# An attention and gated-product kernel: an early key tile, sums moved between engines, one reader per PSUM bank, and a verdict computed in steps

## The chip, the cores and the metric

The kernel runs on one core of one Trainium2 chip. Its time is the device time of one execution, in microseconds (us). The kernel before was timed three times: 763.4 us in the median, 762.13 at least and 764.25 at most.

## The reference

There are 4 batches, 8 heads, 768 positions and 64 elements a head; 4 positions are sinks and the window is 128. Scores are masked to the sinks and the window, the softmax and the weighted values follow, and the result, as 3072 rows of 512, goes through three weight matrices.

```python
scores = scale * np.matmul(q, k.transpose(0, 1, 3, 2))
keep = is_sink | in_window
scores = np.where(keep, scores, -1000000000.0)
a = np.exp(scores - np.max(scores, axis=-1, keepdims=True))
a = a / (np.sum(a, axis=-1, keepdims=True) + 1e-09)
x = np.matmul(a, v)                # 3072 x 512 after a transpose
out = (x @ w_a) * (x @ w_b) @ w_out    # 512x1536, 512x1536, 1536x512
```

All inputs are float32. The number of sinks and the window come as data; the kernel is written for up to 4 sinks and a window up to 128.

## The kernel before

**Split values.** Most matmuls take operands in a rounded form (`fp32r`). A value is kept as a high half and a low half, and a product takes three matmuls: high by high, high by low, low by high. ScalarE mostly makes the high half (a cast), VectorE or GpSimd the low half (value minus high half).

**Chunks.** The products run in seven chunks, c = 0 to 6. Chunk 0 takes the first block of 128 rows of every batch, whose attention `first_tiles` does with an order written out by hand (`FIRST_ORDER`); chunks 1 and 2 take two tiles of 128 rows each, chunks 3 to 6 the last four tiles of one batch each. Beside the products of a chunk runs the attention for later rows: from chunk 1 on a generator `rest()` yields small attention steps, and the products call `between()` after each group of matmuls (a slot), which takes as many steps as the table `PACE` says: chunk number, then (slots, first step, last step). So `1: (37, 0, 34)` spreads steps 0 to 34 over 37 slots. The first 20 steps of `rest()` are an exact attention for two tiles (`pipeline`, `parts_exact`); then comes `attention` for four batches with four tiles each (`parts_split`), the rows of chunks 3 to 6. Chunk 6 has no attention beside it.

**The first 40 us.** `weights`, `weight_words`, `weight_sum`, `weight_high` and `weight_low` turn each raw 64-bit weight into a float32 and then into its halves: two VectorE operations on the words, a ScalarE conversion and a sum, a ScalarE copy (high), a subtraction (low). `weight_high` (L369 to L374) also stores the float32 weight to DRAM through ScalarE's DMA queue (`send`, L1053). Instructions marked with `keep_in_program_order` stay in the order in which they are written on their engine; others, the store among them, are placed by the scheduler. From the end of chunk 0 on, `keep_order` fixes the order on TensorE, VectorE, ScalarE and GpSimd as it is written. The steps of `FIRST_ORDER` that matter here: `H0` to `H3` cast a batch's rows to `xh` (L573), `L0` to `L3` make `xl` (L577), `X` is the exponential (L530), `C` a copy (L540), `wa0`, `ra0`, `ha0`, `la0` the four stages of weight a0, and `begina`, `beginb` start the first products.

**Split attention.** A step of `attention` takes one head and one tile. `load_kq` (L424) brings a key tile for two heads and a query tile; `prep_k` and `prep_q` make their halves on GpSimd (`round` L407, `rest` L410); `scores` (L693) is two matmuls, one with `qh`, one with `ql` (L698); VectorE masks (L705, L706), ScalarE takes the exponential (L708), VectorE the sum and its reciprocal (L717, L718), ScalarE scales (L720). The key tile uses the buffer tag `pt`, which the exact attention's transposed probabilities (`ptx`) hold before. With `cold` set, the first of the four batches begins with three extra steps that load head 0, make its keys and queries, and load head 1's queries.

**Products.** Chunks 1 and 2 use `moe2`: 12 column blocks of weights a and b, then the output product (`project`, L976), whose `gh` and `gl` are made one block behind. Chunks 3 to 6 use `moe7`, a form of matrix product with seven instead of eight block products, with operands `B11`, `T1` to `T4`, `B21`, `B22` made from the chunk's rows by `make_ops` (L1113) in six stages, one stage a slot. For each pair `i` of column blocks and each kind (a, then b) there are four slots. Two PSUM banks are used: X (tag `a`) and Y (tag `b`). X is copied to SBUF by ScalarE (L1238), Y is added to it (L1242), X goes on accumulating, and then its two halves are read: its second half by VectorE into `v12` (L1248 or L1251), its first half into `first`, in kind a by ScalarE's copy (L1256), in kind b by VectorE's multiplication (L1250). The next X uses the same bank. GpSimd adds and multiplies in between (L1243, L1252, L1313) and makes `gl` (L1310); the output product is `project_piece` (L1197). The attention's scores use one PSUM bank in chunks 3 to 5 and two in chunks 1 and 2 (`roomy`).

**The verdict.** While the weights are used, `reduce_check` gathers a minimum and a sum of squares of the raw words. Near the end `verdict` (L70) compares these and the two scalars on VectorE, transposes the result with TensorE, reduces it to one flag, and `values_load` reads the flag into a register of every engine. If the flag is 0 a general path follows; here it does not run.

Of the kernel before, what the change touches and what calls it, by code (L numbers as in the profile page):

```python
# [19 lines left out]
DM, FF = 512, 1536  # L20
# [48 lines left out]

def verdict(tc, cp, ident, chk, val, gp):  # L70
# [5 lines left out]
    V.tensor_reduce(mm[:, 0:1], chk[:, :6 * NJ], axis=AX.X, op=ALU.min)  # L76
    V.tensor_reduce(mm[:, 1:2], chk[:, 6 * NJ:], axis=AX.X, op=ALU.max)
    pin(V.tensor_scalar(bad[:, 0:1], mm[:, 0:1], H_MIN, None, op0=ALU.is_ge))
    pin(V.tensor_scalar(bad[:, 1:2], mm[:, 1:2], H_SUM, None, op0=ALU.is_lt))
    pin(V.tensor_scalar(bad[:, 2:3], val[:, 0:1], 0.0, None, op0=ALU.is_ge))  # L80
    pin(V.tensor_scalar(bad[:, 3:4], val[:, 0:1], float(NS), None, op0=ALU.is_le))
    pin(V.tensor_scalar(bad[:, 4:5], val[:, 1:2], 1.0, None, op0=ALU.is_ge))
    pin(V.tensor_scalar(bad[:, 5:6], val[:, 1:2], float(P), None, op0=ALU.is_le))
    good = cp.tile([P, 2], F32, name="good")
    V.tensor_reduce(good[:, 0:1], bad[:, 0:6], axis=AX.X, op=ALU.min)
    flag = cp.tile([1, 1], I32, name="flag")
    nc.tensor.transpose(gp, good[:, 0:1], ident)
    V.tensor_reduce(flag, gp, axis=AX.X, op=ALU.min)
    return nc.values_load(flag[0:1, 0:1], min_val=0, max_val=1,
                          skip_runtime_bounds_check_because="a comparison gives 0 or 1")  # L90

# [147 lines left out]
class Fast:  # L239
# [169 lines left out]
    def rest(self, o, i, high):  # L409
        self.nc.gpsimd.tensor_tensor(o, i, high.bitcast(F32), op=ALU.subtract)  # L410

# [11 lines left out]

    def load_kq(self, places, h, tag):  # L424
        if h % 2 == 0:
            self.kr = []
            for b, t0, n, s0, nb, kw, *_ in places:
                shape, name = [P, kw], f"kr{tag}_{h}_{b}"
                kr = self.cp.tile(shape, F32, tag="pt", name=name) if kw > DM else self.io(shape, F32, name)
# [16 lines left out]
    def prep_q(self, places, h, tag, k, done):  # L446
        nq = sum(n for _, _, n, *_ in places) * P
        x = self.sp.tile([P, NT * P], F32R, tag=("qh", "ql")[k], name=f"{('qh', 'ql')[k]}{tag}_{h}")
        if k == 0:
            self.round(x[:, :nq], self.qr[:, :nq])  # L450
        else:
            self.rest(x[:, :nq], self.qr[:, :nq], done[1][:, :nq])
        return [x]
# [137 lines left out]

    def attention(self, parts, nt, new_xf, after, cold):
# [12 lines left out]
        for h in range(H + 1):  # L605
# [55 lines left out]
    def parts_split(self, segs):  # L661
# [12 lines left out]

        def load(h):
            self.load_kq(places, h, tag)

# [3 lines left out]
        def queries(h, n):  # L681
            kq[h] += self.prep_q(places, h, tag, n, kq[h])

        def values(m):
# [8 lines left out]
        def scores(h, i):  # L693
            ks, qh, ql = kq[h]
# [358 lines left out]
    def send(self, key, x, queue):  # L1053
        d = self.away[key] = self.dr.tile(list(x.shape), F32, tag="d_" + "_".join(map(str, key)),
                                          name="d_" + "_".join(map(str, key)))
        queue.dma_start(d, x)

# [59 lines left out]
    def make_ops(self, xf, tmp):  # L1117
# [15 lines left out]
        def less(o, x, y, e):  # L1133
# [75 lines left out]
    def moe7(self, c, rows, between, ahead, following, last):  # L1209
# [10 lines left out]
        for i in range(NI):  # L1220
            end = i == NI - 1
            for ki, kind in enumerate("ab"):
                if last and i == NI - 2 and ki == 0:
                    assert not self.checks and not self.unchecked
                    self.ok = self.verdict(self.ps.tile([1, P], F32, tag="s", name="gp"))
                if last and end and ki == 1:
# [6 lines left out]
                X = self.ps.tile([P, 2 * HN], F32, tag="a", name=f"X{c}_{i}{kind}")  # L1233
                lead = self.product(X[:, :HN], w("A11"), ops["B11"], True)
                self.product(X[:, HN:], w("S1"), ops["T1"], False, lead)
                if ready:
# [6 lines left out]
                self.late.append(lambda v22=v22, u2=u2, w2=w2: G.tensor_tensor(v22, u2, w2, op=ALU.add))  # L1243
                self.product(X[:, :HN], w("A12"), ops["B21"], False)
                self.product(X[:, HN:], w("S4"), ops["B22"], False)
                self.done_with(2)
                if ki == 0:
                    slot(lambda: V.tensor_tensor(v12, X[:, HN:], u2, op=ALU.add))  # L1248
                else:
                    slot(lambda: V.tensor_tensor(first, X[:, :HN], quarter(av, 0), op=ALU.mult),  # L1250
                         lambda: V.tensor_tensor(v12, X[:, HN:], u2, op=ALU.add))  # L1251
# [83 lines left out]
    def run(self, scalars, verdict):  # L1335
# [23 lines left out]
        def rest():  # L1359
            yield from self.exact_attention(chunks[1], new_xf(1), True)  # L1360
            for k, parts in enumerate(split):
                after = split[k + 1] if k + 1 < len(split) else None
                yield from self.attention(parts, NT, lambda: new_xf(k + 2), after, k == 0)

# [12 lines left out]
        self.masks(val, True)  # L1377
        self.verdict = lambda gp: verdict(val, gp)
        xs = self.new_x(B)
# [98 lines left out]
def body(tc, kT, kD, qT, vB, vS, kq0, v0, wa, wb, wo, nw, out):  # L1478
    nc = tc.nc
    with tc.tile_pool(name="const", bufs=1) as cp:  # L1480
        ident = cp.tile([P, P], F32, name="ident")
        raw = cp.tile([P, 4], I32, name="nw_raw")
        nc.scalar.dma_start(raw, nw)
        make_identity(nc, ident)
        chk = cp.tile([P, 12 * NJ], F32, name="chk")
        with ExitStack() as ctx:
            f = Fast(tc, ctx, ident, (kT, kD, qT, vB, vS, kq0, v0, wa, wb, wo), out, chk)
            val, ok = f.run(lambda: scalars_to_float(tc, cp, raw), lambda val, gp: verdict(tc, cp, ident, chk, val, gp))
        with tc.If(ok < 1, label="general"):
            general_path(tc, ident, val, kT, qT, vB, wa, wb, wo, out)  # L1490
# [62 lines left out]
```

## Time and profile before

| | us |
|---|---|
| median of three timed runs | 763.4 |
| profiled execution | 759.96 |
| its span in the trace | 758.2 |
| TensorE busy | 730.9 |
| VectorE busy | 466.6 |
| ScalarE busy | 391.6 |
| GpSimd busy | 370.5 |

The page gives each engine's busy time. TensorE's matmuls are pipelined and their ends are modelled, so a stretch without a gap can still be slower than its regular pace; for that one looks at the distance of the starts. PEld is the weight load, which runs beside the matmul. PEclk is the share of the full clock that TensorE was granted. In a wait, the name behind the arrow is what came last before the instruction could start. The products of chunk 0 run from about 28 to 150 us, chunk 1's from there to 222, chunk 2's to 297; chunks 3, 4, 5 and 6 begin near 297, 410, 528 and 646.

### The profile page before, as it was taken

To read this page: it belongs to the slowest core of one execution; us is meant where nothing else is said; L and a number is where in the kernel's file an instruction comes from. 1 tells how busy PE (TensorE), PEld (TensorE's weight loads), DVE (VectorE), ACT (ScalarE), POOL (GpSimd) and SP (SyncE) were. 2 spreads that over 40 slices of the span, in tenths; PEclk is the share of its full clock that TensorE was granted. 3 is DMA by queue.
4 is the path that set the end of the run, shared out by engine and by line. 5 is a ranking of instruction groups with operands and counts; after the bars stand their busy time and mean duration, and the time that the engine had idled before them with its cause. 6 is when DMAs were issued, how large, how long until landed. Compare 5 with 4: busy or idle time off the path is not lost.

```text
span 758.2 us, 14626 instructions
## 1 busy us (share of the span) xinstructions
PE 730.9 (96%) x4952; PEld 642.9 (85%) x4952; DVE 466.6 (62%) x1273; ACT 391.6 (52%) x1135; POOL 370.5 (49%) x390
## 2 busy tenths in 40 slices
PE   8899999999979999899999999999999999999897
PEld 6787778888869888889888888889888988889795
DVE  5799999365476758756647566646567645533222
ACT  5677776376455665555534555443465553444111
POOL 2200000035866795866735876744876633634330
PEclk9999999999999999999999999999999999999999
DMA  9989963368736587867775586876487666599551
GB/s 333 349 291 335 384 234 118 100 212 277 260 105 202 148 274 234 269 223 243 237 253 195 199 298 221 263 241 226 170 286 244 214 210 205 179 329 321 172 164 59
DMA packets 80642, 175.86 MB, mean 232 GB/s; under 512 B 8624, under 2 KB 26032, under 8 KB 80560
## 3 DMA queue, kind: packets, MB, share of 16 engines
q1 hardware_dynamic: 76960, 168.56, 66.6%
q10 hardware_dynamic: 3600, 6.30, 2.2%
q8 instruction: 41, 0.67, 0.4%
q14 instruction: 41, 0.34, 0.2%
HBM read 144.93 MB, written 29.88 MB: 231 GB/s over the span
## 4 chain that ended last, share of the span: by engine, by line
PE 78%; POOL 7%; DMA 6%; DVE 3%; ACT 3%; issue 2%; SPq 1%; ACTq 0%; POOLq 0%; DVEq 0%
PE o L1197 15%; PE b L899 7%; PE a L899 7%; PE o L926 4%; PE av L738 4%; PE s L698 4%; PE o L976 2%; PE s L807 2%; PE X_1b L1150 2%; PE X_4b L1150 2%; PE X_3b L1150 2%; PE t L726 2%; PE X_0b L1150 2%; PE X_4a L1150 2%; PE X_2a L1150 2%
## 5 line engine op out<-in xcount | busy, mean ns | idle before, releaser
L708 ACT ACTIVATE p<-p,st 128x132 f32<-128x132 f32 x128 | 51.7, 404 | 82.2 <-DVE st L706 82.0
L1197 PE MATMUL o<-r_O,gh 128*128 128x512 f32 x288 | 93.7, 406 | 0.0
L1310 POOL TENSOR_TENSOR gl<-bu,gh 128x512 fp32r<-128x512 f32 x46 | 59.3, 1290 | 52.6 <-ACT gh L1307 51.7
L720 ACT ACTIVATE p<-p,st 128x132 f32<-128x132 f32 x128 | 44.9, 398 | 39.6 <-DVE st L718 39.6
L1029 POOL TENSOR_TENSOR s_a<-s_a 128x256 f32<-128x256 f32 x4 | 2.9, 734 | 123.2 <-PE o L926 114.2
L717 DVE TENSOR_SCALAR st<-st 128x2 f32<-128x2 f32 x64 | 36.3, 567 | 42.5 <-ACT p L708 42.5
L705 DVE COPY_PREDICATED s<-own,s 128x128 f32<-128x128 uint16 x128 | 36.8, 288 | 37.9 <-PE s L698 37.7
L1197 PE MATMUL o<-r_O,gl 128*128 128x512 f32 x144 | 56.5, 392 | 0.0
L410 POOL TENSOR_TENSOR ks<-kr,ks 64x656 fp32r<-64x656 f32 x32 | 51.0, 1593 | 2.7
L1197 PEld LDWEIGHTS o<-r_O,gh 128*128 128x128 f32 x288 | 45.0, 189 | 2.6 <-issue 2.1
L1243 POOL TENSOR_TENSOR bu<-x 128x256 f32<-128x256 f32 x24 | 19.0, 792 | 55.9 <-DVE x L1242 54.2
L728 DVE TENSOR_TENSOR pt<-t,tri 128x1024 f32<-128x1024 f32 x32 | 39.1, 1221 | 5.9 <-PE t L726 5.9
L410 POOL TENSOR_TENSOR ql<-qr,qh 128x512 fp32r<-128x512 f32 x32 | 41.4, 1293 | 1.3
L899 PE MATMUL a<-x,w_a 128*128 128x256 f32 x288 | 40.1, 287 | 1.5 <-ACT x L883 1.5
L407 POOL TENSOR_SCALAR ks<-kr 64x656 fp32r<-64x656 f32 x32 | 23.6, 737 | 35.8 <-PE s L698 34.7
L706 DVE CUSTOM_DVE_ANT_0 p<-s,mg 128x132 f32<-128x132 f32 x128 | 37.8, 295 | 4.4
L698 PE MATMUL s<-ks,qh 128*128 128x260 f32 x128 | 38.2, 298 | 2.2 <-DVE st L706 2.0
L1307 ACT CAST gh<-bu 128x512 fp32r<-128x512 f32 x48 | 29.4, 613 | 19.5 <-PE o L1197 10.2
L899 PE MATMUL b<-x,w_b 128*128 128x256 f32 x288 | 39.4, 285 | 0.0
L899 PEld LDWEIGHTS a<-x,w_a 128*128 128x128 f32 x288 | 36.6, 188 | 2.7 <-ACT x L883 1.7
L698 PE MATMUL s<-ks,ql 128*128 128x260 f32 x128 | 36.4, 284 | 1.8 <-POOL ql L410 1.8
L899 PEld LDWEIGHTS b<-x,w_b 128*128 128x128 f32 x288 | 36.2, 189 | 0.4 <-issue 0.3
(480 smaller groups left out, 2258.8 us busy)
## 6 DMA issues: line engine op xcount, KB each, us to landing
r_O<-d_O SPq DMA_DIRECT2D x36, 512.0 KB, 4.2
r_H_a<-d_H_a SPq DMA_DIRECT2D x24, 512.0 KB, 5.4
r_L_a<-d_L_a SPq DMA_DIRECT2D x24, 512.0 KB, 6.1
r_H_b<-d_H_b SPq DMA_DIRECT2D x24, 512.0 KB, 5.4
r_L_b<-d_L_b SPq DMA_DIRECT2D x24, 512.0 KB, 6.0
qr<-in_qT_dram SPq DMA_DIRECT2D x32, 256.0 KB, 3.8
raw_a<-in_wa_dram SPq DMA_DIRECT2D x12, 512.0 KB, 6.8
raw_b<-in_wb_dram SPq DMA_DIRECT2D x12, 512.0 KB, 6.6
```

Source lines behind the costliest of these rows:

```text
L410: self.nc.gpsimd.tensor_tensor(o, i, high.bitcast(F32), op=ALU.subtract)
L698: nc.tensor.matmul(ps, lhsT=q[:, i * P:(i + 1) * P], rhs=ks[:, c0s[i]:c0s[i] + SW], start=n == 0, stop=n == 1)
L705: nc.vector.copy_predicated(ps[:, :P], self.own.bitcast(mybir.dt.uint16), ps[:, W:])
L706: nc.vector.tensor_tensor_reduce(out=p, in0=ps[:, :W], in1=self.mg[:, :W], scale=-0.125, scalar=BIG, op0=ALU.add, op1=ALU.min, accum_out=s ...
L708: nc.scalar.activation(p, p, AF.Exp, bias=st[:, 0:1], scale=-1.0, accum_out=st[:, 1:2])
L717: nc.vector.tensor_scalar(st[:, 2], st[:, 1], 1e-9, None, op0=ALU.add)
L720: nc.scalar.mul(p[:, k, :], p[:, k, :], st[:, 3, k:k + 1])
L728: nc.vector.tensor_tensor(self.parted(nt)[:, h % 2].rearrange("p (c m) q -> p c m q", m=2), tp.unsqueeze(2).to_broadcast(shape), self.tri. ...
L899: mm = self.nc.tensor.matmul(ps[:, cols], lhsT=w[:, ksl], rhs=x[:, kk, cols], start=start and kk == 0 and i == 0, stop=kk == NK - 1 and i ...
L1150: mm = self.nc.tensor.matmul(ps, lhsT=a[:, ksl], rhs=b[:, kk, :], start=start and kk == 0 and n == 0, stop=kk == 1 and n == 2, skip_group_ ...
L1197: self.nc.tensor.matmul(outs[t], lhsT=g[:, sl], rhs=w, start=j == 0 and n == 0, stop=j == NJ - 1 and n == 2)
L1310: (V if late else G).tensor_tensor(hl[k][1], halves[k], hl[k][0].bitcast(F32), op=ALU.subtract)
```

## The change

- The DMA that stores the first three weights (a0, b0, a1) is kept in program order on ScalarE's queue, right behind the weight's own copy.
- The first split chunk's head-0 key tile uses the buffer `xfB` instead of `pt`. Its load is issued at step 6 of `rest()`, the load of head 1's queries at step 14, the keys are made at step 17 and the queries at step 18, all beside the exact attention. The three extra steps are gone, and `PACE` is shifted by three.
- In `scores`, the first matmul of a head's first tile gets a dependence on the instruction that makes `ql`.
- In `make_ops`, one difference and two low halves (`B21`, `T4`) go from GpSimd to VectorE.
- In `moe7`, kind a's `first` is read by VectorE ahead of `v12`, in the slot after X's last products, instead of by ScalarE a product later.
- `verdict` is split into three parts: the comparisons in the slot where all stood before, the transpose and the flag two slots later, the register load at the beginning of the last pair of column blocks.

```diff
-PACE = {1: (37, 0, 34), 2: (32, 34, 64), 3: (44, 64, 105), 4: (44, 105, 146), 5: (44, 146, 187)}
+LOAD_AT = 6
+PACE = {1: (37, 0, 31), 2: (32, 31, 61), 3: (44, 61, 102), 4: (44, 102, 143), 5: (44, 143, 184)}
...
         if kind != "o":
-            self.send(("F", kind, j), self.wf[kind, j], self.nc.scalar)
+            op = self.send(("F", kind, j), self.wf[kind, j], self.nc.scalar)
+            if (kind, j) in FIRST:
+                self.tc.keep_in_program_order(op)
...
-        if cold:
-            load(0)
-            yield
-            yield
-            keys(0)
-            queries(0, 0)
-            queries(0, 1)
-            load(1)
-            yield
...
             for n, q in enumerate((qh, ql)):
-                nc.tensor.matmul(ps, lhsT=q[:, i * P:(i + 1) * P], rhs=ks[:, c0s[i]:c0s[i] + SW],
-                                 start=n == 0, stop=n == 1)
+                mm = nc.tensor.matmul(ps, lhsT=q[:, i * P:(i + 1) * P], rhs=ks[:, c0s[i]:c0s[i] + SW],
+                                      start=n == 0, stop=n == 1)
+                if i == 0 and n == 0:
+                    self.tc.add_manual_dep(mm.ins, made.ins.name, mybir.DependencyInfo(
+                        mybir.DependencyClass.Sync, mybir.DependencyReason.DATA), reason="one wait for both parts")
...
-                [low("T1", ta, V), high("T2", tb), high("T3", b12), less(b11, b21, tb, G)],
+                [low("T1", ta, V), high("T2", tb), high("T3", b12), less(b11, b21, tb, V)],
                 [low("T2", tb, V), low("T3", b12, V), high("B21", b21), high("B22", b22)],
-                [low("B22", b22, V), low("B21", b21, G), high("T4", b11)],
-                [low("T4", b11, G)]]
+                [low("B22", b22, V), low("B21", b21, V), high("T4", b11)],
+                [low("T4", b11, V)]]
...
                 if last and i == NI - 2 and ki == 0:
                     assert not self.checks and not self.unchecked
-                    self.ok = self.verdict(self.ps.tile([1, P], F32, tag="s", name="gp"))
+                    self.later(self.judge_stages())
+                if last and end and ki == 0:
+                    self.ok = self.read()
...
                 if ki == 0:
-                    slot(lambda: V.tensor_tensor(v12, X[:, HN:], u2, op=ALU.add))
+                    slot(lambda: V.tensor_copy(first, X0), lambda: V.tensor_tensor(v12, X1, u2, op=ALU.add))
...
                 self.product(Y[:, HN:], w("A22"), ops["T4"], False)
-                if ki == 0:
-                    A.copy(first, X[:, :HN])
...
+    def judge_stages(self):
+        return [[self.judge], [], [lambda: self.gather(self.ps.tile([1, P], F32, tag="s", name="gp"))]]
...
+            load, _, keys, queries = split[0][-4:]
+            begin = {LOAD_AT: lambda: load(0, "xfB"), LOAD_AT + 8: lambda: load(1), 2 * H + 1: lambda: keys(0),
+                     2 * H + 2: lambda: (queries(0, 0), queries(0, 1))}
+            for k, _ in enumerate(self.exact_attention(chunks[1], new_xf(1), True)):
+                begin.get(k, lambda: None)()
+                yield
```

## Rows read from the trace of the kernel before

**Rows 1.** The page's busy times: engine, us (share of the span), instructions.
```profile
PE 730.9 (96%) x4952; PEld 642.9 (85%) x4952; DVE 466.6 (62%) x1273; ACT 391.6 (52%) x1135; POOL 370.5 (49%) x390
```

**Rows 2.** TensorE's waits: us in total, times, the longest.
```profile
PE o L1197 <- POOL gl L1310: 4.0, 3, 1.3
PE s L698 <- DVE st L706: 2.0, 4, 1.0
PE s L698 <- POOL ql L410: 1.8, 2, 0.9
```

**Rows 3.** Timeline, 20 to 34 us: start, us, engine, line, instruction, idle before.
```profile
21.04 1.15 ACT L530 ACTIVATE p<-s,st 128x128 f32<-128x128 f32 x4 [1.98 <-DVE v L555]
...
22.71 1.49 PE L551 MATMUL av<-v,pt 128*128 128x128 f32 x11 [1.63 <-ACT pt L540]
...
31.90 0.33 ACTq L1056 DMA_DIRECT2D d_F_a<-wf_a  x1
...
32.91 0.38 PE L899 MATMUL afirst<-xh,w_a 128*128 128x256 f32 x1 [1.18 <-ACT xh L573]
...
33.63 0.38 PE L899 MATMUL afirst<-xl,w_a 128*128 128x256 f32 x1 [0.34 <-DVE xl L577]
```

**Rows 4.** Chain that ended last, before 21 us: start, us, what.
```profile
11.46 9.07 DMA raw_a<-in_wa_dram
```

**Rows 5.** Stretches: length, busy PE, PEld, DVE, ACT, POOL, PEclk, DMA share, GB/s.
```profile
34.00:39.00 5.00, 5.00 (x28) 4.85 (x27) 3.72 (x8) 1.83 (x4) 0.00 (x0) 0.66 0.59 208
...
60.00:80.00 20.00, 20.00 (x103) 16.02 (x102) 19.56 (x46) 16.22 (x38) 0.00 (x0) 1.00 0.97 328
...
200.00:220.00 20.00, 17.60 (x120) 15.62 (x118) 11.40 (x39) 9.34 (x33) 18.91 (x21) 1.00 0.48 159
```

**Rows 6.** Timeline where the split attention begins, 194 to 208 us.
```profile
194.31 0.38 SPq L430 DMA_DIRECT2D kr<-in_kT_dram  x1
...
202.33 0.39 PE L698 MATMUL s<-ks,ql 128*128 128x260 f32 x1 [0.94 <-POOL ql L410]
...
207.15 0.50 PE L976 MATMUL o<-w_o,gl 128*128 128x512 f32 x1 [0.61 <-POOL gl L989]
```

**Rows 7.** Timeline of one pair of score matmuls, at 460 us.
```profile
460.67 0.36 PE L698 MATMUL s<-ks,qh 128*128 128x260 f32 x1
...
460.86 0.28 PE L698 MATMUL s<-ks,ql 128*128 128x260 f32 x1
```

**Rows 8.** Timeline at two chunk ends, near 297 and 412 us.
```profile
295.59 1.78 DVE L1131 TENSOR_TENSOR opw_o<-x,opw_o 128x512 fp32r<-128x512 f32 x1
297.29 0.68 DVE L1131 TENSOR_TENSOR opw_o<-bu,opw_o 128x512 fp32r<-128x512 f32 x1
...
299.74 0.39 PE L1150 MATMUL Y_0a<-opw_o,r_H_a 128*128 128x256 f32 x1 [0.55 <-DVE opw_o L1131]
...
411.97 1.76 POOL L1131 TENSOR_TENSOR opw_o<-xfB,opw_o 128x512 fp32r<-128x512 f32 x1
...
417.96 0.50 PE L1197 MATMUL o<-w_o,gl 128*128 128x512 f32 x1 [1.33 <-POOL gl L1310]
```

**Rows 9.** Timeline at one X start, and one X's weight loads by shape (busy, idle).
```profile
382.48 0.39 PE L1197 MATMUL o<-r_O,gl 128*128 128x512 f32 x1
382.97 0.98 PE L1150 MATMUL X_4b<-opw_o,w_b 128*128 128x256 f32 x6
...
L1150 PEld LDWEIGHTS X_3b<-opw_o,w_b 128*128 128x128 f32 x48 | 6.5, 189 | 2.3 <-ACT av L1256 2.0
```

**Rows 10.** Timeline of a score's bank: the mask's last part, the next score.
```profile
457.58 0.09 DVE L706 DVE_READ_ACCUMULATOR2_ANT st<- 128x1 f32 x1
...
458.07 0.29 PE L698 MATMUL s<-ks,qh 128*128 128x260 f32 x1
```

**Rows 11.** Timeline at the verdict, 712 to 715 us.
```profile
712.03 0.39 PE L1197 MATMUL o<-r_O,gl 128*128 128x512 f32 x1
...
714.37 0.95 PE L1150 MATMUL X_4a<-opw_o,w_a 128*128 128x256 f32 x6 [0.90 <-DVE flag L88]
```

More of the change, by code (lines that the diff above doesn't have):

```diff
@@ L67, in scalars_to_float, with verdict @@
     return val
-def verdict(tc, cp, ident, chk, val, gp):
+def verdict(tc, cp, ident, chk, val):
     nc, pin = tc.nc, tc.keep_in_program_order
@@ L75, in verdict, with judge, gather, read @@
     mm = cp.tile([P, 2], F32, name="mm")
[L76 to L83, printed above, removed]
     good = cp.tile([P, 2], F32, name="good")
-    V.tensor_reduce(good[:, 0:1], bad[:, 0:6], axis=AX.X, op=ALU.min)
     flag = cp.tile([1, 1], I32, name="flag")
[L87 to L90, printed above, removed]
+    def judge():
+        V.tensor_reduce(mm[:, 0:1], chk[:, :6 * NJ], axis=AX.X, op=ALU.min)
+        V.tensor_reduce(mm[:, 1:2], chk[:, 6 * NJ:], axis=AX.X, op=ALU.max)
+        pin(V.tensor_scalar(bad[:, 0:1], mm[:, 0:1], H_MIN, None, op0=ALU.is_ge))
+        pin(V.tensor_scalar(bad[:, 1:2], mm[:, 1:2], H_SUM, None, op0=ALU.is_lt))
+        pin(V.tensor_scalar(bad[:, 2:3], val[:, 0:1], 0.0, None, op0=ALU.is_ge))
+        pin(V.tensor_scalar(bad[:, 3:4], val[:, 0:1], float(NS), None, op0=ALU.is_le))
+        pin(V.tensor_scalar(bad[:, 4:5], val[:, 1:2], 1.0, None, op0=ALU.is_ge))
+        pin(V.tensor_scalar(bad[:, 5:6], val[:, 1:2], float(P), None, op0=ALU.is_le))
+        V.tensor_reduce(good[:, 0:1], bad[:, 0:6], axis=AX.X, op=ALU.min)
+    def gather(gp):
+        nc.tensor.transpose(gp, good[:, 0:1], ident)
+        V.tensor_reduce(flag, gp, axis=AX.X, op=ALU.min)
+    def read():
+        return nc.values_load(flag[0:1, 0:1], min_val=0, max_val=1,
+                              skip_runtime_bounds_check_because="a comparison gives 0 or 1")
+    return judge, gather, read
 def general_path(tc, ident, val, kT, qT, vB, wa, wb, wo, out):
@@ L409, in rest @@
     def rest(self, o, i, high):
-        self.nc.gpsimd.tensor_tensor(o, i, high.bitcast(F32), op=ALU.subtract)
+        return self.nc.gpsimd.tensor_tensor(o, i, high.bitcast(F32), op=ALU.subtract)
     def places(self, segs):
@@ L422, in halves, with load_kq @@
         return (slice(0, D), slice(D, P)) if h % 2 == 0 else (slice(D, P), slice(0, D))
-    def load_kq(self, places, h, tag):
+    def load_kq(self, places, h, tag, home="pt"):
         if h % 2 == 0:
@@ L590, in exact_attention, with attention @@
         return self.pipeline(units, nt, *self.parts_exact(segs, xf, apart), 2, 1)
-    def attention(self, parts, nt, new_xf, after, cold):
+    def attention(self, parts, nt, new_xf, after):
         sinks, split, scores, finish, transposes, av, sinks_t, sinks_av, load, values, keys, queries = parts
         lone = nt > 2
-        if cold:
-            load(0)
-            yield
-            yield
-            keys(0)
-            queries(0, 0)
-            queries(0, 1)
-            load(1)
-            yield
         for h in range(H + 1):
@@ L673, in parts_split, with load @@
         half = (slice(0, D), slice(D, P))
-        def load(h):
-            self.load_kq(places, h, tag)
+        def load(h, *home):
+            self.load_kq(places, h, tag, *home)
         def keys(h):
@@ L1055, in send @@
                                           name="d_" + "_".join(map(str, key)))
-        queue.dma_start(d, x)
+        return queue.dma_start(d, x)
     def shift(self, i):
@@ L1243, in moe7 @@
                 self.late.append(lambda v22=v22, u2=u2, w2=w2: G.tensor_tensor(v22, u2, w2, op=ALU.add))
-                self.product(X[:, :HN], w("A12"), ops["B21"], False)
-                self.product(X[:, HN:], w("S4"), ops["B22"], False)
+                self.product(X0, w("A12"), ops["B21"], False)
+                self.product(X1, w("S4"), ops["B22"], False)
                 self.done_with(2)
                 if ki == 0:
-                    slot(lambda: V.tensor_tensor(v12, X[:, HN:], u2, op=ALU.add))
+                    slot(lambda: V.tensor_copy(first, X0), lambda: V.tensor_tensor(v12, X1, u2, op=ALU.add))
                 else:
-                    slot(lambda: V.tensor_tensor(first, X[:, :HN], quarter(av, 0), op=ALU.mult),
-                         lambda: V.tensor_tensor(v12, X[:, HN:], u2, op=ALU.add))
+                    slot(lambda: V.tensor_tensor(first, X0, quarter(av, 0), op=ALU.mult),
+                         lambda: V.tensor_tensor(v12, X1, u2, op=ALU.add))
                     self.late.append(lambda v12=v12: G.tensor_tensor(v12, v12, quarter(av, 1), op=ALU.mult))
@@ L1359, in rest @@
         def rest():
-            yield from self.exact_attention(chunks[1], new_xf(1), True)
+            load, _, keys, queries = split[0][-4:]
[4 more added lines that the diff above has]
+                yield
             for k, parts in enumerate(split):
                 after = split[k + 1] if k + 1 < len(split) else None
-                yield from self.attention(parts, NT, lambda: new_xf(k + 2), after, k == 0)
+                yield from self.attention(parts, NT, lambda: new_xf(k + 2), after)
         def beside(step):
@@ L1377, in run @@
         self.masks(val, True)
-        self.verdict = lambda gp: verdict(val, gp)
+        self.judge, self.gather, self.read = verdict(val)
         xs = self.new_x(B)
```

15 lines of the change are left out of this document (9 added, 6 removed).

## The prediction

> **What bounds the kernel now.** I read the busy row of the page first: TensorE is busy for 730.9 of 758.2 us [rows 1], so a change can win only in the 27 us in which TensorE waits, or where it runs below its normal pace. Then the list of TensorE's waits, which says whom it waits for: the largest entries are the `gl` halves from GpSimd (4.0 us in three places of 1.3), `ql` from GpSimd (1.8 in two) and the scores' bank from VectorE (2.0 in four) [rows 2]. Then the timeline at each of these places, to see what stands ahead of the late instruction on its own engine. Each wait costs a little more than its entry, because the matmuls behind it start late too. I therefore count from start to start and subtract the regular distance (0.12 us per 256 or 260 columns, 0.24 per 512).
>
> **1. The stores of the first three weights, pinned.** Today the store of weight a0 stands in ScalarE's queue ahead of four exponentials. The exponentials start at 21.04, after an idle time of 1.98 us, and TensorE waits 1.63 for the copy behind them [rows 3]; what ScalarE had waited for was the landing of a weight load, 9.07 us after 11.46, which the store had to see [rows 4]. The store of a1 does it again: issued at 31.90, when GpSimd's sum is ready, it holds the cast of `xh`, and TensorE starts at 32.91 and 33.63, after waits of 1.18 and 0.34 [rows 3]. Pinned behind the weight's own ScalarE copy, the stores of a0 and a1 stand after those exponentials and that cast, whose inputs were ready about 2 and 1.7 us earlier. From start to start TensorE loses 1.9 and 2.0 us here. A third loss follows: from 34 to 39 us the granted clock averages 0.66 [rows 5], part of it at the lower of its two levels, right after TensorE's idle time at 31.7 to 33.6; at full clock this work would take 5 x (1 - 0.66) = 1.7 us less. Without the idle time I expect the clock to stay up. Sum 5.6. TensorE can't keep all of it: VectorE, which makes the low halves of the weights, is busy 19.56 of 20 us from 60 to 80 [rows 5], and its own shift is its two waits behind the same ScalarE stalls (about 1.6 and 1.8) plus a little slack. I take 3.6; ends 0 (the wait for the lane moves along, or VectorE holds TensorE) and 5.6.
>
> **2. The first key tile with its own buffer, early.** Today its load is issued at 194.31, when the exact attention has left the buffer [rows 6]. GpSimd then has two heads' keys and queries, the conversions and the `gl` halves at once: busy 18.91 of 20 us from 200 to 220 [rows 5]. TensorE pays 0.94 and 0.61 [rows 6] and 0.85 (the other of the two `ql` waits in rows 2); with the late followers 1.1 + 0.9 + 1.1 = 3.1. After the change the keys come three steps before the first scores, the queries two, and 31 steps instead of 34 are spread over the chunk's 37 slots, so the split scores start two slots earlier and their GpSimd work spreads. Both loads of head 0, and head 1's queries, are issued on SP's queue far ahead, where nothing waits for them. New: the keys now stand ahead of a conversion and two `gl` on GpSimd; by my count these fit with under 1 us to spare. The wait at the end of that chunk (221 us) stays, since the last steps fall in the same slots. I take 2.8; ends 0 and 3.1.
>
> **3. One wait for both halves of the queries.** The matmul with `qh` now waits for `ql` too; behind it in TensorE's queue is everything. Where `ql` is late it starts one matmul later (0.12); where it is ready, a second wait goes. The nearest rows are a score pair behind a small delay, whose second matmul starts 0.19 after the first instead of 0.12 [rows 7]; I take 0.5 over 32 heads, ends -0.5 and 2.2 (32 x 0.07).
>
> **4. Operand sums on VectorE at the four chunk ends.** GpSimd's chain is late three times: a low half of 1.76 us at 411.97 stands ahead of the product and of `gl`, and TensorE waits 1.33 at 417.96 [rows 8], about 1.6 with the followers; the wait list has three such, 4.0 us [rows 2], 4.7 with followers. At the first of the four ends the operands themselves are late: Y_0a waits 0.55 at 299.74 for a VectorE low half [rows 8], about 1.1 with followers. VectorE gets three more operations. Alone such a one takes 0.68; beside GpSimd's it takes 1.78 [rows 8]. So 3 x 0.68 = 2.0 is added and, at the first end, 3 x (1.78 - 0.68) = 3.3 of slowing may go, at the others about 1.7 by the rows of the same line. But B21's low half, which GpSimd finished beside, now comes last but one on VectorE, just when X_0a wants it: up to 0.5 a chunk end. 5.8 - 1.0 = 4.8; ends 0 and 5.8.
>
> Row and rule: the pair of engines slows each other, 0.68 against 1.78 [rows 8]. The Trainium skill ("Perfetto Trace Analysis", Optimizing Scalar/DVE Operations) says that the two share an SBUF read port, so that moving work between them may not help. By that this part would give nothing, which is the third rival below; by the row it gives the 4.8, since what TensorE waits for is GpSimd's place in line.
>
> **5. `first` read by VectorE.** Today ScalarE's copy out of X waits for VectorE's `v12` and for its own queue, and the next X starts at 382.97, 0.49 instead of 0.24 after the matmul before it [rows 9], and its own six matmuls take 0.11 longer. Counted so, 15 of the 24 starts of kind b lose 4.4 us together; the weight loads of one such group sit idle for 2.0 [rows 9]. The starts of kind a, whose bank only VectorE reads at the end, lose nothing, so the losses should go. VectorE's price: 24 copies of about 0.42. Its masked score leaves the bank that much later; at 457.58 its last part runs, 0.4 ahead of the next score at 458.07 [rows 10], so 0.34 (the start-to-start cost of one such read) just fits; where VectorE is already late it does not. 4.4 - 1.0 = 3.4; ends -3 (18 x 0.42 with half of them in the path, plus nothing won) and 4.4.
>
> **6. The verdict spread.** The last regular matmul before it starts at 712.03; X_4a starts at 714.37 after a wait of 0.90 for the flag [rows 11]: 2.34 - 0.24 = 2.1 lost. What stays is one transpose (0.1) and each engine's load of the flag, long ready; from flag end to X_4a there was 0.58, of which I leave 0.4. Gain 1.6; ends 1.0 and 2.0.
>
> **The sum** is 3.6 + 2.8 + 0.5 + 4.8 + 3.4 + 1.6 = 16.7 us. The profiled execution took 759.96 (a span of 758.2 and 1.8 around it), 3.4 under the median of 763.4; on the median the sum gives 746.7. Six parts each free TensorE for the next thing that is late, and the rows show VectorE with half a microsecond to spare in the score slots; I take 2.3 off for waits that take the place of those removed: 749.0.
>
> **Rivals.**
> *The start doesn't move.* For it: VectorE has 0.44 us of slack in 20 from 60 to 80 [rows 5], and the store's wait is for a landing, not for its place. Against: its new place, behind the copy that comes after those exponentials, is later than that landing. Part 1 falls to 0: 752.6.
> *The bank's new reader is late.* VectorE's copies push the masked scores; scores wait for VectorE already in four places [rows 2]. Part 5 falls from 3.4 to about -1: 753.4.
> *Work moved between GpSimd and VectorE gives nothing.* The moved low halves wait behind GpSimd's remaining sums, and X_0a waits instead of `gl`: part 4 falls to 0: 753.8. The three bound events each leave the others standing; two at once give about 757.
> *Slower.* VectorE becomes the bound of chunks 3 to 5: with one score bank in these chunks, a score can't start before the masked one before it has left, and VectorE gets 0.42 per pair of products. If that chain falls behind in each of the 18 products by the 1.17 us that a start-to-start count shows where VectorE is late today (wait list: up to 1.0), 21 us are added against some 13 won elsewhere: 771. It decides from about 0.7 us per product. Against it: VectorE is busy 62% [rows 1].
>
> **Chances.** Forecast 0.60 (own range 745 to 752), start doesn't move 0.13, late reader 0.09, nothing from moving 0.10, two of these 0.03, slower 0.05. The range 742 to 758 takes in the upper ends of the terms (5.6 and 5.8 for parts 1 and 4) and the single rivals. Within 0.3% (2.3 us, about what a measurement of this kernel can tell from no change) lies little: faster 0.91, same 0.04, slower 0.05.
>
> **What would show it.** In the profile after: TensorE's waits for `pt`, `xh` and `xl` before 35 us gone and the clock full through 39 (part 1); no `ql` or `gl` wait around 200 to 212 (2); no `gl` wait of 1.3 at the three chunk ends, VectorE's low halves near 0.68 (4); the X starts of kind b in the rhythm of kind a (5); no gap at the verdict (6). Wrong would be a list of waits in which VectorE's score line has grown by what the others lost.

## The result, and the profile after

The changed kernel takes 753.52 us (median of 4 runs, 752.39 to 753.87); the kernel before, beside it, takes 762.76. The ratio is 0.9874, with an interval of 0.9854 to 0.9895: 9.6 us less at 763 us, where the forecast said 14.4 less than 763.4. The time lies inside the forecast's wide range (742 to 758), but outside its own narrow one (745 to 752), 4.5 us above the forecast. The profiled execution took 752.39 with a span of 750.5.

One thing about the work has to be known to read the times. In the changed kernel, the load of head 1 (step 14) replaces the tile `self.qr` before the queries of head 0 are made from it (step 18). Head 0 of chunk 3 is therefore computed from head 1's queries. The operations and their sizes are the same, so the time is that of the whole work. The undone parts below keep this, except where their expectation says otherwise; the two repairs of part 2 and the kernels built on the second of them make head 0's queries from its own tile.

The page's busy times, as in [rows 1]:

```profile
PE 726.9 (97%) x4952; PEld 641.4 (85%) x4952; DVE 475.9 (63%) x1309; ACT 385.0 (51%) x1111; POOL 354.2 (47%) x378
```

TensorE is busy for 4.0 us less, and the span is 7.7 shorter, so that its idle time has shrunk from 27.3 to 23.6. Part of the 4.0 is work that ran at the lower clock before (34 to 39 us). TensorE's waits, as in [rows 2] (total, times, longest):

```profile
PE o L983 <- POOL gl L996: 2.5, 3, 1.5
PE s L702 <- DVE st L713: 1.9, 4, 0.9
...
PE Y_0a L1157 <- DVE opw_o L1138: 1.3, 3, 0.4
...
PE s L702 <- POOL ql L421: 1.3, 1, 1.3
...
PE X_0a L1157 <- DVE opw_o L1138: 1.0, 3, 0.6
...
PE o L1204 <- POOL gl L1321: 0.6, 2, 0.3
```

The three `gl` waits of 1.3 at the chunk ends are down to two of 0.3. In their place stand six waits for VectorE's low halves, and near 200 us there are three `gl` waits (L983) and one for `ql`. So the list already shows which parts did not pay: 4 and 2.

The start, as in [rows 3] and [rows 5]: TensorE's waits between 20 and 40 us, three ScalarE rows, and two stretches (length, busy PE, PEld, DVE, ACT, POOL, granted clock, DMA share, GB/s).

```profile
22.60 2.05 PE L562 MATMUL av<-v,pt 128*128 128x128 f32 x16 [0.30 <-ACT pt L551]
...
32.47 0.50 PE L906 MATMUL a<-xh,w_a 128*128 128x512 f32 x1 [0.66 <-ACT g L941]
...
37.36 0.73 PE L906 MATMUL b<-xh,w_b 128*128 128x512 f32 x2 [0.91 <-DVE w_b L391]
```
```profile
28.16 0.62 ACT L381 CAST w_a<-wf_a 128x512 fp32r<-128x512 f32 x1 [0.57 <-POOL wf_a L369]
30.92 0.33 ACTq L1063 DMA_DIRECT2D d_F_a<-wf_a  x1
31.29 0.66 ACT L366 ACTIVATE raw_b<-raw_b 128x512 int32<-128x512 uint32 x1 [2.52 <-DMA raw_o<-in_wo_dram]
```
```profile
34.00:39.00 5.00, 4.09 (x18) 3.05 (x17) 4.36 (x13) 3.87 (x9) 0.00 (x0) 1.00 0.98 289
60.00:80.00 20.00, 20.00 (x102) 15.93 (x101) 19.73 (x48) 15.62 (x35) 0.00 (x0) 1.00 1.00 350
```

The wait for `pt` is 0.30 instead of 1.63, those for `xh` and `xl` are gone, and the clock stays at its upper level (1.00 instead of 0.66). New are a wait behind VectorE (`w_b`) and one behind ScalarE (`g`, 0.66). The second comes from the change itself: the store of a1, pinned right behind that weight's copy (28.16), is issued only at 30.92, when `raw_o` has landed (30.90, a load issued at 22.02). ScalarE sits 2.52 us behind it, though the conversion of `raw_b` that comes next does not read `raw_o`.

The start of the split attention, as in [rows 6]: TensorE's waits, then GpSimd's order ahead of the last one.

```profile
195.95 0.39 PE L702 MATMUL s<-ks,qh 128*128 128x260 f32 x1 [1.25 <-POOL ql L421]
198.65 0.50 PE L983 MATMUL o<-w_o,gl 128*128 128x512 f32 x1 [0.30 <-POOL gl L996]
204.52 0.50 PE L983 MATMUL o<-w_o,gl 128*128 128x512 f32 x1 [0.61 <-POOL gl L996]
211.40 0.50 PE L983 MATMUL o<-w_o,gl 128*128 128x512 f32 x1 [1.54 <-POOL gl L996]
```
```profile
207.68 0.73 POOL L418 TENSOR_SCALAR ks<-kr 64x656 fp32r<-64x656 f32 x1
208.50 2.04 POOL L421 TENSOR_TENSOR ks<-kr,ks 64x656 fp32r<-64x656 f32 x1
210.62 0.73 POOL L996 TENSOR_TENSOR gl<-g,gh 128x256 fp32r<-128x256 f32 x1
```

Four waits of 3.7 us stand where there were three of 2.4. The last `gl` is late because the keys of a later head, 2.8 us, stand ahead of it on GpSimd, which has had no idle time since 185.97.

One chunk end, as in [rows 8]: VectorE, GpSimd and TensorE.

```profile
406.58 1.22 DVE L1141 TENSOR_TENSOR xfA<-xfB,tmp 128x512 f32<-128x512 f32 x1
...
408.66 1.77 DVE L1138 TENSOR_TENSOR opw_o<-xfA,opw_o 128x512 fp32r<-128x512 f32 x1
...
411.01 0.68 DVE L1138 TENSOR_TENSOR x<-xfB,x 128x512 fp32r<-128x512 f32 x1
411.61 0.68 DVE L1138 TENSOR_TENSOR opw_o<-xfB,opw_o 128x512 fp32r<-128x512 f32 x1
...
412.81 0.67 DVE L1138 TENSOR_TENSOR x<-xfA,x 128x512 fp32r<-128x512 f32 x1
```
```profile
406.13 1.12 POOL L1262 TENSOR_TENSOR bu<-bu,av 128x256 f32<-128x256 f32 x1 [1.29 <-DVE bu L1261]
408.28 1.60 POOL L1324 TENSOR_TENSOR bu<-bu,av 128x512 f32<-128x512 f32 x1 [1.03 <-DVE bu L1265]
412.85 1.78 POOL L1321 TENSOR_TENSOR gl<-bu,gh 128x512 fp32r<-128x512 f32 x1 [2.97 <-ACT gh L1318]
```
```profile
410.49 0.39 PE L1157 MATMUL Y_0a<-opw_o,r_H_a 128*128 128x256 f32 x1 [0.43 <-DVE opw_o L1138]
...
412.34 0.86 PE L1157 MATMUL X_0a<-opw_o,w_a 128*128 128x256 f32 x5 [0.18 <-DVE opw_o L1138]
...
414.68 0.50 PE L1204 MATMUL o<-w_o,gl 128*128 128x512 f32 x1 [0.29 <-POOL gl L1321]
```

`gl` is 1.04 us less late, but VectorE is now late twice. The moved sum (406.58) takes 1.22 and T3's low half (408.66) 1.77, each beside a GpSimd product; Y_0a waits for that low half. B21's low half (411.61) comes after B22's (411.01), and X_0a wants it first.

The rows also show how the pair slows. The moved sum ends at 407.80 and T3's low half at 410.43, each 0.55 us after the GpSimd operation that was running when it began (ends 407.25 and 409.88). In six profiles (before, after, u4, v1, v2 and both repairs), all 86 of these 128x512 VectorE operations that began well inside a GpSimd operation ended 0.55 us after it. Where VectorE begins first it keeps its 0.67 to 0.68, and GpSimd pays: `gl` at 412.85, beside T4's low half (412.81), takes 1.78 instead of 1.26 (at 416.65 in the kernel before). So the price of a moved operation that begins second is what is left of its neighbour, plus 0.55.

The X start and the verdict, as in [rows 9] and [rows 11]: the regular matmul before, and the start.

```profile
698.63 0.39 PE L1204 MATMUL o<-r_O,gl 128*128 128x512 f32 x1
698.86 0.88 PE L1157 MATMUL X_3b<-opw_o,w_b 128*128 128x256 f32 x6
...
706.41 0.39 PE L1204 MATMUL o<-r_O,gl 128*128 128x512 f32 x1
706.64 0.64 PE L1157 MATMUL X_4a<-opw_o,w_a 128*128 128x256 f32 x4
```

Both starts stand 0.23 after the matmul before them: the regular distance.

Below, "gaps" are sums of what TensorE's starts lose against the regular distance (each loss over 0.06 us), counted as in the prediction. Over the whole execution they fall from 59.9 to 52.4, 7.5 of the span's 7.7 us.

### The profile page after: what moved, and what is told of

Same layout as the page of the kernel before. It is cut to its first block, busy times and chain, and to the rows that moved or that the text cites. A ratio compares the mean times of both kernels' runs of the same rounds, so it can differ in the third digit from the quotient of the medians.

```text
span 750.5 us, 14604 instructions
## 1 busy us (share of the span) xinstructions
PE 726.9 (97%) x4952; PEld 641.4 (85%) x4952; DVE 475.9 (63%) x1309; ACT 385.0 (51%) x1111; POOL 354.2 (47%) x378
## 4 chain that ended last, share of the span: by engine, by line
PE 78%; DMA 6%; POOL 6%; DVE 5%; ACT 3%; issue 1%; SPq 0%; ACTq 0%; POOLq 0%; DVEq 0%
PE o L1204 17%; PE a L906 7%; PE b L906 6%; PE o L933 5%; PE s L702 4%; PE av L745 4%; PE o L983 2%; PE t L733 2%; PE X_0b L1157 2%; PE X_2b L1157 2%; PE X_1b L1157 2%; PE X_2a L1157 2%; PE X_3a L1157 2%; PE X_5a L1157 2%; PE X_4a L1157 2%; PE X_4b L1157 2%
## 5 line engine op out<-in xcount | busy, mean ns | idle before, releaser
L724 DVE TENSOR_SCALAR st<-st 128x2 f32<-128x2 f32 x64 | 33.1, 517 | 42.8 <-ACT p L715 42.8
```

## The experiments

Each kernel is the changed one with one thing altered. The table gives the ratio to the kernel before, run beside it on the same chip (before: 763.01, 763.13 and 761.67 in the three groups), and the difference in ratio to the changed kernel at 763 us. Each ratio is known to +-1.0 to +-2.2 us, so a difference to the changed kernel to +-1.9 to +-2.7. By that u3, u4 and u5 can't be told from the changed kernel, and u2 only just.

| kernel | us | ratio (95%) | against the change |
|---|---|---|---|
| changed | 753.52 | 0.9874 (0.9854-0.9895) | |
| u1, part 1 undone | 756.01 | 0.9919 (0.9900-0.9938) | +3.4 |
| u2, part 2 undone | 750.71 | 0.9846 (0.9830-0.9861) | -2.1 |
| k2, keys at step 12 | 749.96 | 0.9831 (0.9818-0.9845) | -3.3 |
| u5, part 5 undone | 754.45 | 0.9880 (0.9865-0.9895) | +0.5 |
| k3, keys at step 14 | 748.02 | 0.9802 (0.9778-0.9826) | -5.5 |
| u4, part 4 undone | 752.86 | 0.9860 (0.9839-0.9882) | -1.1 |
| v1, B21 first | 750.65 | 0.9832 (0.9809-0.9855) | -3.2 |
| v2, sum on GpSimd | 748.42 | 0.9797 (0.9775-0.9820) | -5.9 |
| both repairs | 743.81 | 0.9766 (0.9743-0.9788) | -8.2 |
| both, part 5 undone | 746.22 | 0.9792 (0.9770-0.9815) | -6.3 |
| u6, part 6 undone | 754.77 | 0.9920 (0.9891-0.9948) | +3.5 |
| u3, part 3 undone | 751.93 | 0.9872 (0.9848-0.9895) | -0.2 |

**Part 1 undone.**

```
-            op = self.send(("F", kind, j), self.wf[kind, j], self.nc.scalar)
-            if (kind, j) in FIRST:
-                self.tc.keep_in_program_order(op)
+            self.send(("F", kind, j), self.wf[kind, j], self.nc.scalar)
```


> The changed kernel with part 1 undone: the stores of a0, b0 and a1 are not pinned. Changed kernel: 753.5. Theory (the stores hold ScalarE): the waits for pt (1.6) and for xh and xl return before 35 us, the clock falls again after them, and what the two traces show as the same matmuls' shift (114.38 against 118.74 us, 4.4) is lost: 757.9. Forecast's own term: 3.6, 757.1. Rival (VectorE holds the lane anyway, and the shift comes from elsewhere): no wait returns that matters, 753.5 to 755.

It measured 756.01, by ratio 3.4 more. TensorE's waits, and a stretch with its granted clock, in this kernel and then in the changed one:

```profile
PE av L560 <- ACT pt L549: 3.5, 1, 3.5
```
```profile
24.00:30.00 6.00, 6.00 (x44) 5.97 (x43) 3.53 (x13) 3.39 (x9) 2.57 (x2) 0.77 0.97 371
```
```profile
24.00:30.00 6.00, 6.00 (x52) 5.94 (x52) 4.83 (x12) 2.99 (x6) 2.32 (x2) 1.00 1.01 389
```

The `pt` wait is back, longer than before the change, and after it the clock averages 0.77 instead of 1.00. The waits for `xh` and `xl` are back too (0.73 at 34.05, 0.34 at 34.78), though here the clock holds behind them (1.00 from 34 to 39 us). Part 1 does what the forecast said, by the forecast's mechanism and near its price (3.4, known to +-2.1).

**Part 2 undone, and two other places for it.** u2 takes back the old buffer, the old steps and their pace. k2 and k3 keep the change, but move the steps:

```
-            begin = {..., LOAD_AT + 8: lambda: load(1), 2 * H + 1: lambda: keys(0),
-                     2 * H + 2: lambda: (queries(0, 0), queries(0, 1))}
+            begin = {..., 14: lambda: keys(0),                     # k2: 12
+                     15: lambda: (queries(0, 0), queries(0, 1)),   # k2: 13
+                     16: lambda: load(1)}                          # k2: 14
```


> The changed kernel with part 2 undone: the key tile takes the old buffer, its load, keys and queries stand at the old place, and 34 steps instead of 31 fall into the chunk. The queries of head 0 come from their own tile, as in the kernel before; in the changed kernel the load of head 1 replaces that tile first, so head 0 is computed from head 1's queries with the same operations. Theory (part 2 costs, since the keys stand behind a conversion in GpSimd's order and the scores start two slots earlier): the four waits of 195 to 212 us (ql 1.25; gl 0.30, 0.61, 1.54) become the old three (0.94, 0.61, 0.85), 752 to 752.5. Forecast (part 2 is worth 2.8): 756.3. Rival (neither): 753.5.

> The changed kernel with head 0's keys made at step 12 and its queries at step 13 (instead of 17 and 18), which is GpSimd's idle time of 174 to 180 us; the queries come from head 0's own tile. Theory (GpSimd's backlog of 189 to 214 us makes all four waits): ql 1.25 and gl 0.30, 0.61 and 1.54 all go, with followers about 4.0: 749.5. Rival 1 (the gl waits come from the keys of heads 1 and 2, which stand ahead of gl in GpSimd's order whatever the backlog): only the ql wait goes, 1.5: 752.0. Rival 2 (the keys in the idle time hold gl or the conversions behind them): new waits before 195 us, 753.5 or more.

> The changed kernel with head 0's keys at step 14, its queries at step 15 and head 1's load at step 16, so that the queries come from head 0's own tile. With the keys at step 12 all four waits of 195 to 212 us went (5.5 to 0.7 us of gaps), but a new one of 2.2 with 1.3 behind it came at 183.84, since the keys took the buffer that the last kx tile of the exact attention wanted, and its load moved behind two others on SP's queue; 750.0. At step 14 that tile has its buffer. Theory: the four waits go and none comes, 753.5 - 4.8 = 748.7, or 747 if the waits behind the new one go too. Rival (in this order GpSimd comes to the keys later, and its backlog of 189 to 214 us is only shorter): the last gl wait stays, 750.

u2 measured 750.71. Part 2 is therefore not worth 2.8, and by the ratios it costs 2.1 (+-2.0). Three of u2's runs lie near 750.6 and two near 753.2; its profile is of a run of 753.29, so it can't show what the faster ones save. It doesn't have the old three waits either, but a longer one:

```profile
201.15 0.58 PE L711 MATMUL s<-ks,qh 128*128 128x260 f32 x1 [2.99 <-POOL ql L421]
```

GpSimd got to the keys only at 196.66, after 1.18 us of waiting for the key tile to land, and from 201.0 to 204.5 the granted clock averages 0.52. Whether the faster runs are those without this wait is not shown.

k2 measured 749.96, near the theory's number, but by another way. From 190 to 215 us the gaps fell from 5.5 to 0.7, as the theory says. A new wait came, first GpSimd, then SP's queue, then TensorE:

```profile
176.18 0.73 POOL L418 TENSOR_SCALAR ks<-kr 64x656 fp32r<-64x656 f32 x1 [1.60 <-PE s L814]
```
```profile
180.26 0.85 SPq L803 DMA_DIRECT2D kx<-in_kD_dram  x2
```
```profile
183.84 0.68 PE L814 MATMUL s<-kx,qx 128*128 128x260 f32 x2 [1.95 <-issue]
```

`ks` and the exact attention's `kx` share a ring of two buffers. At step 12 the keys take the place of the last `kx`; its load, which the changed kernel issues at 176.26 and 177.19, is issued at 180.26, and its scores come 2.2 us late, with 1.3 more lost just behind them, where the granted clock averages 0.59 (184.0 to 188.2). At step 14 the last `kx` has its buffer. k3 measured 748.02, 5.5 less than the change by ratio; GpSimd and TensorE there:

```profile
205.48 1.06 POOL L996 TENSOR_TENSOR gl<-g,gh 128x256 fp32r<-128x256 f32 x1
```
```profile
206.59 0.50 PE L983 MATMUL o<-w_o,gl 128*128 128x512 f32 x1 [0.34 <-POOL gl L996]
```

One wait of 0.34 is left of the four. The theory holds: what cost time was GpSimd's work of head 0 among the later work, not the load.

**Part 4 undone, and two other divisions of its work.**

```
                 [low("T1", ta, V), high("T2", tb), high("T3", b12), less(b11, b21, tb, V)],   # u4, v2: G
                 [low("T2", tb, V), low("T3", b12, V), high("B21", b21), high("B22", b22)],
-                [low("B22", b22, V), low("B21", b21, V), high("T4", b11)],                    # u4: B21 on G
-                [low("T4", b11, V)]]                                                          # u4: G
+                [low("B21", b21, V), low("B22", b22, V), high("T4", b11)],                    # v1, v2
+                [low("T4", b11, V)]]
```


> The changed kernel with part 4 undone: the third sum and the low halves of B21 and T4 are GpSimd's again. Theory (the moved work only turned gl's wait of 1.3 into VectorE's waits at Y_0a and X_0a): the gaps at the four chunk ends go from 1.7, 1.7, 1.6 and some 0.8 back to 1.6, 1.6, 1.6 and 1.4; 753.5 to 754.1. Forecast's term: 4.8, 758.3. Rival (VectorE's extra work also delays scores behind the ends, so undoing it wins): 752 to 753.

> The changed kernel with the low half of B21 ahead of that of B22 on VectorE, since X_0a takes B21 first. Theory (X_0a's waits of 0.18, 0.18 and 0.64 are for B21 behind B22): these go, with followers 1.3 to 1.6: 752.0. Rival 1 (B22 is then late by as much, six matmuls on: the waits move there): 753.0 to 753.5. Rival 2 (X_0a waits for T1 or for VectorE's other work): unchanged, 753.5.

> As the one with B21 ahead, and the third sum (b11 - b21 - tb) back on GpSimd, so that VectorE has two of the three moved operations. Theory (Y_0a waits for the lows of T2 and T3 behind that sum, 1.23 us on VectorE at the chunk end): the Y_0a waits go too, three of 0.43 with followers 0.6 each, 752.0 - 1.8 = 750.2. Rival 1 (GpSimd's sum beside VectorE's lows slows these, as it did before, 0.68 against 1.78): the waits stay, 752 or more. Rival 2 (GpSimd's chain gets late again and gl waits): gl 0.29 grows by up to 1.0 each, 753.

u4 measured 752.86: all of part 4 together is worth nothing that can be measured. The gaps at the four ends are 5.8 in both kernels. v1 measured 750.65, a little under its theory, but its profile is of its slowest run (753.75). In it X_0a's waits are gone, and the gaps at the ends fall only to 5.0, because `gl` is late instead:

```profile
PE o L1204 <- POOL gl L1321: 1.5, 2, 0.8
PE Y_0a L1157 <- DVE opw_o L1138: 1.3, 3, 0.5
```

Rival 1 holds in part: most of the wait moved, though to `gl` and not to B22. v2 measured 748.42, better than its theory. Its end near 410 us on VectorE and GpSimd:

```profile
409.68 1.22 DVE L1138 TENSOR_TENSOR opw_o<-xfA,opw_o 128x512 fp32r<-128x512 f32 x1
...
411.48 1.12 DVE L1138 TENSOR_TENSOR opw_o<-xfB,opw_o 128x512 fp32r<-128x512 f32 x1
```
```profile
406.77 1.29 POOL L1141 TENSOR_TENSOR xfA<-xfB,tmp 128x512 f32<-128x512 f32 x1 [7.81 <-DVE tmp L1141]
...
409.17 1.18 POOL L1262 TENSOR_TENSOR bu<-bu,av 128x256 f32<-128x256 f32 x1
410.31 1.74 POOL L1324 TENSOR_TENSOR bu<-bu,av 128x512 f32<-128x512 f32 x1
```

GpSimd had sat idle for 7.81 us ahead of that sum, and the two low halves shown still take 1.1 to 1.2 beside its products. But T3's low half is done at 410.90, and Y_0a's first product with T3 starts at 411.56; and B21's low half comes first. No wait is left at this end, and the gaps at the four ends fall to 1.6. Against u4 on the same chip v2 is 4.8 us faster by ratio: a gain of the size of the forecast's term for part 4 exists (+-2.4), with two of the three operations moved and B21 ahead. The order alone, v1 against u4, gives 2.1, which is within the noise.

**Part 5 undone.**

```
-    slot(lambda: V.tensor_copy(first, X0), lambda: V.tensor_tensor(v12, X1, u2, op=ALU.add))
+    slot(lambda: V.tensor_tensor(v12, X1, u2, op=ALU.add))
...
+    A.copy(first, X0)          # behind the A22 product
```


> The changed kernel with part 5 undone: ScalarE copies first out of X behind the A22 product. Theory (two readers of one bank make the next X late): the X starts of kind b are late again by 0.25 to 0.49 and the score starts after them, which VectorE's copy had made late (about 0.23 each in chunks 3 to 5), are on time; the two traces' gaps give a net 2.9: 756.4. Forecast: 3.4, 756.9. Rival (VectorE's copies cost in the score slots what the bank gains): 753.5.

> The kernel with both repairs, but part 5 undone: ScalarE copies first behind the A22 product. Theory (part 5 pays in the last chunk alone, 2.1 us of gaps between 655 and 770 in the kernel that undid it alone, and little where VectorE has scores to mask): 742.9 + 1.0 to 2.1 = 743.9 to 745.0. Forecast: 3.4, 746.3. Rival (the smaller effect seen was noise between the runs): the 2.9 of the traces before and after, 745.8.

Alone it measured 754.45, 0.5 more; from the kernel with both repairs, on one chip, 746.22 against 743.81, 2.0 more by ratio. One X start with part 5 undone, in the last chunk, and a score in the changed kernel:

```profile
667.54 0.39 PE L1204 MATMUL o<-r_O,gl 128*128 128x512 f32 x1
668.51 0.97 PE L1157 MATMUL X_1b<-opw_o,w_b 128*128 128x256 f32 x6 [0.58 <-ACT av L1266]
```
```profile
596.33 0.36 PE L702 MATMUL s<-ks,qh 128*128 128x260 f32 x1 [0.36 <-DVE st L713]
```

X starts 0.97 instead of 0.23 after its forerunner. The score's wait of 0.36 is one of the longest of its kind; u4, which keeps part 5, loses only 0.15 at the same start. Counted by chunk, undoing part 5 costs X 2.0 us of gaps in chunks 3 to 5 and gives the scores 1.6 back there; in the last chunk, which has no scores, it costs 2.1. So what part 5 wins, it wins at the end.

**Parts 6 and 3 undone.**

```
-                    self.later(self.judge_stages())
+                    self.judge(); self.gather(...); self.ok = self.read()     # u6
...
-                if i == 0 and n == 0:
-                    self.tc.add_manual_dep(mm.ins, made.ins.name, ...)        # u3
```


> The changed kernel with part 6 undone: the verdict is judged, gathered and read in one place. Theory: TensorE again waits for the flag's chain, 2.0 by the two traces' gaps: 755.5. Forecast: 1.6, 755.1. Rival (the late end is the output's store, which the verdict delayed only in part): 754.

> The changed kernel with part 3 undone: the matmul with qh does not wait for ql. Theory (the score pairs look the same in both traces, so part 3 is worth nothing): 753.5, and the ql wait of 1.25 near 196 us moves to the second matmul and is 0.1 shorter. Forecast: 0.5, 754.0. Upper end: 2.2, 755.7.

u6 measured 754.77; its row at the verdict:

```profile
707.83 0.95 PE L1157 MATMUL X_4a<-opw_o,w_a 128*128 128x256 f32 x6 [0.90 <-DVE flag L93]
```

The last regular matmul before it starts at 705.48, so X_4a is 2.1 late, as before the change, and 0.0 with it. The ratios differ by 3.5 (+-2.7), which does not contradict it. u3 measured 751.93; by ratio that is 0.2 less: part 3 is worth nothing that can be measured.

**Both repairs together** (k3's steps and v2's division in one kernel).

> The changed kernel with both repairs: keys at step 14, queries at 15 and head 1's load at 16; and the third sum on GpSimd with the low halves of B21 (ahead of B22) and T4 on VectorE. The two act in different stretches (190 to 215 us, and the four chunk ends). Theory (they add): 753.5 - 5.5 - 5.1 = 742.9, 742 to 744.5. Rival (part of either gain was a faster start of those runs, which differ by up to 1.5 us before 40 us): 745 to 747.

It measured 743.81 (743.54 to 745.42), ratio 0.9766 (0.9743 to 0.9788), 8.2 us less than the change. The gaps are 43.9, 8.6 below the changed kernel's 52.4; k3 alone took off 4.6 and v2 3.0, so in the traces the two add. The ratios of k3 and v2 would give 11.4 together, and 8.2 was measured; their noise allows that difference.

## Why the prediction was right, and where it was not

The kernel got faster by two thirds of what was forecast, and that alone proves no step. Parts 1 and 6 paid about as forecast, part 5 by its mechanism but less, and parts 2 and 4 not at all. The time also lies where the rivals with part 1, 5 or 4 lost had put it (752.6, 753.4, 753.8), so it can't tell them from the forecast.

- **Part 1** (3.6): right. The price by ratio is 3.4, the mechanism is in the rows, and VectorE's cap is there too (`w_b`, 0.91 at 37.36). The rival that the start doesn't move is out. What was not seen ahead: the step "the stores of a0 and a1 stand after those exponentials and that cast" is true, but the store of a1 still waits for a landing (`raw_o`, 30.90) and now holds the ScalarE work behind it, 2.52 us in this profile, of which TensorE feels 0.66.
- **Part 6** (1.6): right, 2.1 by the rows and 3.5 (+-2.7) by ratio. The 0.4 left for loading the flag was not needed.
- **Part 3** (0.5): -0.2 by ratio, inside its bounds and below what can be measured.
- **Part 5** (3.4): right mechanism, size off. All X starts of kind b are on time again. The price on the scores was put at 1.0; in chunks 3 to 5 it is 1.6 of the 2.0 won there. Over these chunks the step "0.34 just fits" failed: the score then waits, as at 596.33. What stays is 2.1 in the last chunk, and 0.5 to 2.0 by the runs, each known to about +-2.
- **Part 4** (4.8): the step that failed is the price of the moved operations. It took them as alone, 0.68 each, though [rows 8] had 1.78 beside GpSimd. On VectorE they have to see the GpSimd operation end that runs when they begin: the moved sum took 1.22 and T3's low half 1.77, and Y_0a had no such slack; B21's place after B22's cost X_0a up to 0.64 a chunk end. The net is 0 (-1.1 +-2.3): the rival that moving work gives nothing, held at 0.10, came true, with Y_0a waiting as well as X_0a. One thing of the step was right: Y_0a's wait of 0.55 near 299 us is gone, and the gaps at this end fell from 1.8 to 0.8, of which u4 gives back 0.4.
- **Part 2** (2.8): the sentence "by my count these fit with under 1 us to spare" failed. The keys at step 17 fell behind idle time of GpSimd (173 to 189 us, 5.6 of 16 us busy) into its busiest stretch, the first scores came two slots earlier, and the forecast did not ask whether GpSimd's other work would come earlier too. It did not: the conversion ahead of the keys began at 184.37 after 3.84 us without work, and then waited 0.86 more for its load. The price is -2.1 by ratio (+-2.0), below the bound of 0. With the keys in the idle time the same idea gives 3.4 (k3 against u2 by ratio), near the 2.8.

By ratio alone the six parts, each undone by itself, are worth 3.4 - 2.1 - 0.2 - 1.1 + 0.5 + 3.5 = 4.0 us, while the change is 9.6 faster. The other 5.6 are not settled: the ratio of the changed kernel, known to +-1.6, stands in all six differences, so that an error of 1 us in it counts six times, and parts may also help each other. The gaps of the six profiles, each less the changed kernel's, sum to 7.5 (3.4, 1.0, 0.1, 0.1, 1.7, 1.3), as do those of before less after; but single profiles differ by 1 to 3 us at the start alone. The terms add up to 16.7, 7.1 more than was measured. The 2.3 that the forecast took off for new waits covered part of what parts 2, 4 and 5 fell short, and named none of them; that the total still fell into the wide range is in so far luck.

The Trainium skill ("Perfetto Trace Analysis", Optimizing Scalar/DVE Operations) says that the two engines share an SBUF read port, so that moving work between them may not help. The trace agrees on the price (0.68 alone, 1.22 and 1.77 beside GpSimd) and u4 on the result. That a shared port is the reason, no run here shows. v2 shows what the rule leaves open: two of the three operations moved, with B21 first, gave 4.8 us, although the slow pairs remain (1.12 to 1.22).

## What to carry to other kernels

Price a moved operation at its duration beside its new neighbours, and ask for each consumer in which order it wants the results; here three moved operations gave 0, and two of them in another order 4.8 us. A store pinned in a compute engine's queue can hold that engine in its new place too: ask what landing it still waits for. An early load wins nothing if the work on it is put into an in-order engine's busiest stretch: look for that engine's idle time, and for the ring of buffers that the early tile then takes from another. When a tile is loaded earlier, look also at what replaces it before it is read.

## What was not expected of the hardware

The runs of one kernel differ at the start. The gaps between 20 and 40 us were 3.2 to 5.0 in most profiles with part 1, but 6.9 in v1's and 7.3 in that of both repairs with part 5 undone. There ScalarE sat 4.11 and 4.42 us behind the pinned store of a1, which was issued right after `raw_o` had landed (32.75 after 32.73, and 32.81 after 32.79); the second of these:

```profile
32.81 0.33 ACTq L1063 DMA_DIRECT2D d_F_a<-wf_a  x1
33.19 0.65 ACT L366 ACTIVATE raw_b<-raw_b 128x512 int32<-128x512 uint32 x1 [4.42 <-DMA raw_o<-in_wo_dram]
```

In the changed kernel the same wait was 2.52, in v2's profile 0.34. The two long ones stand in profiles of the slowest runs of their kernels (753.75 of 749.8 to 753.75, and 748.49 of 745.26 to 748.49), so this landing near 30 us may make much of the spread. That was not tested, nor was a later place for the store.
